# A frozen instruction order, turns on quarters of the array, and a first quad loaded by hardware queues

## The chip, the cores and the metric

The kernel runs on one core of a Trainium2 chip. A core has a matrix engine (TensorE, PE in the profile; PEld is its loading of weights), a vector engine (VectorE, DVE), a scalar engine (ScalarE, ACT), GpSimd (POOL) and SyncE (SP). Each engine works through its own list of instructions in order and waits on semaphores for the others. Data come from memory (HBM) into on-chip memory by DMAs. A DMA is issued either by POOL, through a queue whose descriptors are made in software and which can change fp32 to bf16 on the way, or by SP and ACT, through hardware queues, which copy the numbers as they are. Matrix products land in PSUM, which has eight banks of 128 x 512 fp32 numbers, and are copied out by DVE or ACT.

The metric is the device time of one execution in microseconds (us).

## The reference

```python
def _attn_ref(q, k, v):                      # 8 batches, 12 heads, 448 tokens, 64 numbers per head
    scores = scale * np.matmul(q, k.transpose(0, 1, 3, 2))
    attn = np.maximum(scores, 0.0) ** 2 / S
    return np.matmul(attn, v)

def _moe_ref(x, w_gate, w_val, w_out):       # x is the attention's output, 3584 x 768
    gate = np.maximum(x @ w_gate, 0.0)       # 768 x 1536
    val = x @ w_val                          # 768 x 1536
    return gate * val @ w_out                # 1536 x 768
```

There is no softmax: a score becomes relu(score) squared, and the sum over keys needs no other normalisation. So each block of keys can be finished by itself, and all scale factors move to the end.

## The kernel before

**Attention.** Heads are worked on in quads, four heads of one batch; a batch has three quads (0, 1, 2). Of a quad, queries lie in partitions 0 to 63 of a tile, keys in 64 to 127, with seven slots of 64 tokens each. A *turn* is a transpose on PE (a matrix product with the identity, `ident`) that brings the 64 numbers of a head into the partitions, so that scores can be computed; it lands in PSUM and DVE or ACT copies it to `qkT`. For each slot of keys PE computes the scores of all queries (L686), DVE or ACT takes the relu out of PSUM (L699, L697) and squares it (L711, L709), and PE multiplies by the values (L728); the result goes to `xT` (L744, L746). Products of 64 rows and 64 columns of weights use a quarter of PE's array, and four quarters can work at once.

The first batch is split in two halves of the queries (192 and 256), so that the feed-forward part can begin early. Its quads are turned by L540 (first half of the queries and the keys) and L547 (the other queries), those of batch 1 by L588, 28 turns of 128 tokens' worth of columns per quad with the full 128 partitions as rows, so that query and key slots turn together. Batches 2 to 7 are turned by DMAs on SP's queue, from a rearranged copy (`perm`, L610 or L612).

**Feed-forward.** Batches 0 and 1 use plain products with the gate and value weights (L793). From batch 2 on, pairs of batches use seven products in place of eight (Strassen's scheme in Winograd's form, L902), with sums and differences made on DVE and copies of PSUM (L849 on ACT, L853 on DVE). The output product is done in the same way (L1017, copies L851 and L855), and stored from SP's queue, at the end from ACT's too (L989).

**Loads.** All inputs come through POOL's queue (L404), changed to bf16 on the way; at most eight are under way. Only the first half of the queries of quad 0 of batch 0 comes as fp32 by the hardware queues of ACT and SP (L455) and is changed to bf16 on DVE (L457).

**Order.** While the program is built, a planner (`Planner`, `plan`) decides what each engine does and when. PE's order and that of the loads are written out as strings of letters (`PE_ORDER`, `LOAD_ORDER`); a third string (`AHEAD`) shifts the ranks of DVE's and ACT's operations. The planner prices each operation with costs that are written in the code, takes the one that can start first, and so settles the engine of an operation that DVE or ACT could do, and the bank or buffer of each result. Where its calendar has a hole on PE in the first 32 us, it puts in *fillers*: products of ones (L1171) that nobody reads. An operation's emitted place on its engine is all that remains of the calendar; the chip runs the lists as they stand, with semaphores between them.

Of the kernel before, what the change touches and what calls it, by code (L numbers as in the profile page):

```python
# [15 lines left out]
class Res:  # L16


    def __init__(self, n):
        self.free = {i: 0.0 for i in range(n)}  # L20
        self.by = {}

    def at(self, i):

        t, op = self.free[i], self.by.get(i)
        return t if op is None else max(t, op.end + Planner.LATE[1])


class Buf:


    def __init__(self, res, among=None, width=1):
        self.res, self.width = res, width
        self.among = among if among is not None else sorted(res.free)
        self.readers, self.last, self.idx = 0, 0.0, None

    def pick(self, now=0.0):

        best = None
        for i in self.among:  # L40
            if all(i + w in self.res.free for w in range(self.width)):
                t = max(self.res.at(i + w) for w in range(self.width))
                if best is None or max(t, now) < max(best[0], now):
                    best = (t, i)
        return best


class Op:


    def __init__(self, engs, emit, deps=(), alloc=(), reads=(), mode=None, grp=None):
        self.engs, self.emit = engs, emit
        self.deps, self.alloc, self.reads = list(deps), list(alloc), list(reads)
        self.mode, self.grp = mode, grp
# [4 lines left out]
        self.start = self.end = self.eng = None  # L59
        for b in self.reads:  # L60
            b.readers += 1


class Planner:
    NOUT = 8
    SWITCH = 0.1
    BIAS = 0.2
    MARGIN = 1.5
    LATE = (2.0, 1.0, 0.3)
    TO_LOAD, LOADED = 2.35, 0.95  # L70
    TO_TURN, TURNED, TURN = 1.7, 0.8, 3.65
    ISSUE = 0.28
    TO_HW = 1.9
    COLD = 4.6, 1.6
    FILL_FROM = 0.4
    FILL_COLD = 5.5
    FILL_UNTIL = 32.0
    FILL_MARGIN = 0.1
    GV_ORDER = '1256734'
    OUT_ORDER = 'ab1cd572364'  # L80
    END_ORDER = ('517364', '523')
    BUFFERS = (3, 11, 3, 4, 4, 4, 3)
    PV_PAIRS = (0, 0)
    JOIN = True
    TWO_QUEUES = True
    SPLIT = False
    MERGE = False
    URGENT = {'sh': -0.5, 'perm': 0.5}
    YIELD = {'sq': 0.1, 'sh': 0.1}
    PV_AT_0 = 0  # L90
    QT = 3
    PART = 6
    PV_AT = (1, 1)
    T_AT = (1, 1)
    MORE_UNTIL = 6
    BY_PE = 6
    ORDER = 'LV610ab2c3x4oy5rzqp'

    def __init__(self, banks):
        self.banks = banks  # L100
        self.t = {"POOL": 1.25, "DVE": 0.85, "ACT": 0.74, "SP": 0.74}
        self.ops = []
        self.mode = None
        self.dma_t = 0.0
        self.queues = [], []
        self.loads = []

    def free_at(self, bank):
        return self.banks.free.get(bank, 1e9)

    def now(self, op):
        return self.t.get("PE", 0.0) if "PE" in op.engs else 0.0

    def ready(self, op):
        r = 0.0
        for d in op.deps:
            if d.end is None:
                return None
            if d.eng != "PE" or "PE" not in op.engs:
                r = max(r, d.end + (self.LATE[0] if d.xbar else self.LATE[2] if d.load else 0.0))  # L120
        for b in op.alloc:
            p = b.pick(self.now(op))
            if p is None:
                return None
            r = max(r, p[0])
        return r

    def best(self, op):
        r = self.ready(op)
        if r is None:  # L130
            return None
        c = None
        for e, (occ, busy) in op.engs.items():
            if e in ("DVE", "ACT"):
                r = max([r] + [d.end + self.MARGIN for d in op.deps if d.load and not d.hw])
            s = max(r, self.t.get(e, 0.0))
            if e == "PE" and op.mode != self.mode:
                s = max(r, self.t.get(e, 0.0) + self.SWITCH)
            f = s + busy + (self.BIAS if e == "DVE" and len(op.engs) > 1 else 0.0)
            if c is None or f < c[0]:  # L140
                c = (f, s, e)
        return c[1], c[2], r

    def rates(self, a, b):

        if not (a and b):
            return 1.0, 1.0
        share = a[0][0].share
        return 1.0 - share, share

    def flow(self, a, b, t, until):
        while t < until and (a or b):
            rates = self.rates(a, b)
            d = min([q[0][1] / r for q, r in zip((a, b), rates) if q] + [until - t])
            t += d
            for q, r, post in zip((a, b), rates, (self.LOADED, self.TURNED)):
                if q:
                    q[0][1] -= d * r
                    if q[0][1] < 1e-6:
                        q.pop(0)[0].end = t + post  # L160
        return t

    def transfer(self, queue, op, arrival, work):


        self.dma_t = max(self.flow(*self.queues, self.dma_t, arrival), arrival, self.dma_t)
        self.queues[queue].append([op, work])
        self.flow(*([list(x) for x in q] for q in self.queues), self.dma_t, 1e9)

    def commit(self, op, s, e):  # L170
        assert op.behind is None or op.behind.start is not None
        op.start, op.eng = s, e
        occ, busy = op.engs[e]
        if e == "PE" and s < self.COLD[0] and op.kind != "fill":
            occ, busy = occ * self.COLD[1], busy * self.COLD[1]
        now = self.now(op)
        self.t[e] = s + occ
        op.end = s + busy
        if e == "PE":
            self.mode = op.mode  # L180
        if op.hw:
            self.transfer(0, op, s + self.TO_HW, op.load)
        elif op.load:
            self.loads.append(op)
            self.transfer(0, op, s + (op.to or self.TO_LOAD), op.load)
        elif op.xbar:
            self.transfer(1, op, s + self.TO_TURN, self.TURN)
        else:
            op.end += op.land
        for b in op.alloc:  # L190
            t, b.idx = b.pick(now)
            assert t <= s + 1e-6
            for w in range(b.width):
                del b.res.free[b.idx + w]
                b.res.by.pop(b.idx + w, None)
            b.last = op.end
        for b in op.reads:
            b.readers -= 1
            b.last = max(b.last, op.end + (self.LATE[1] if op.land or op.xbar else 0.0))
            if b.readers == 0:  # L200
                for w in range(b.width):
                    b.res.free[b.idx + w] = b.last
                    if op.xbar:
                        b.res.by[b.idx + w] = op
        self.ops.append(op)
# [3 lines left out]
PE_ORDER = (  # L209
    'aaaccdabaabcbdafjabbaebbbaacdfhafcBBADDaabbabgaZLBKMBAccabaGCFFFCFFdagbaJJebjHHbbaAEFaadEcaaGBCBAAggcbaAFLDGFA'  # L210
    'PGGbaaCCCACgfcccBEbbaGEEDACedcccCCbbaDAfgAbbacBDCaaAAAhccbCCbaBCAaAadBeAabacBJbaDBACBDGcBFAAFAACBHAAGBAFBBCBAA'
    'BDfaAADaaCCAAcBBABaaABBAacbabDAGDAEABBCAIEAEACABAAcACbaAACAGAabbBABaaBCADAecbEACAaAFebaBACEAabEEFAfaBFgaCAabdA'
    'CbbaGBAdeCBecdCAaaaAAAABaebaAEKADBAQCBADADABAAAbaDBAbbBDAAACacFBAaabFBACCGCCABcbaCDBAADEbbaEABCAIBBAdIAAbdHFAA'
    'CaaDACCCaJACBABCBBfbaBABaccAACADbaAAAAadaaICAcaAAaaABAaabaBBbaaCEIACaFKBAAJABBAACABAAABCBBBACBCDCBAABAAAADADHC'
    'BDCBICHABCFBHACAFEBEHBABCAEGBBDBBDCCECAAAGBABBABBBCGEAABBCBCCBABBABBBA'
)
LOAD_ORDER = (
    'aaaaaafcbaakaacaaedbbbthbcabkacccefhbdiggaggaacddaaeebfdbecaccacabfdebcgagbaaeabhabddeaacejejafacacaammkbddbbf'
    'dacabba'
)  # L220
AHEAD = (
# [7 lines left out]
    'iirisnnpmtmbhgjmliojiqibnfpmqnlhmqlkrqirmgnrkbhgmfkfhiinjolmbgnpgnrmjpouoqjmdqqivtssxbolmfhoqpqtqnnligsktopkqu'  # L229
    'kminsgnsiljkjruqjolqoplphilpnnigmrljomgnipnnpismjkkoqnlkpgikmkmknkjingpnqkmojsnklmkjrqmpmklhgknllfrlgqkjknmlfj'  # L230
    'nrrmpslmrmnnnikmonninkjmmmqjlikpqqmnjohpijopklkn'
)

def arranged(ops, letters, base):

    left, out = list(ops), []
    for c in letters:
        out.append(left.pop(ord(c) - ord(base)))  # L240
# [1044 lines left out]
```

## Time and profile before

| | |
|---|---|
| runs | 403.94, 406.0 and 1019.69 us; median 406.0 |
| span of the profiled execution, first to last instruction | 402.3 us |
| own time of the profiled execution | not listed apart from the span; the runs shown at 403.94 and 406.0 lie 1.6 and 3.7 us above it |
| PE busy | 393.8 us, 98% |
| DVE busy | 326.1 us, 81% |
| ACT busy | 274.0 us, 68% |
| POOL busy | 75.7 us, 19% |
| bytes moved by DMA | 43.54 MB, mean 108 GB/s |
| mean granted clock of PE | 0.990 |

The run of 1019.69 us lies far outside and is left out of what follows.

How to read the profile: the span runs from the first to the last instruction. A busy time is the time in which an engine has at least one instruction running; PE's instructions overlap, so a busy PE is not a PE at its peak. The clock row gives the share of PE's full clock that was granted in each fortieth of the span. The chain that ended last is followed back from the last instruction, at each step to what released it. In a table of stretches each row gives start and end, length, busy time of each engine with the number of its instructions, the granted clock, the mean busy share of the 16 DMA engines, and GB/s.

### The profile page before, as it was taken

To read this page: it belongs to the slowest core of one execution; us is meant where nothing else is said; L and a number is where in the kernel's file an instruction comes from. 1 tells how busy PE (TensorE), PEld (TensorE's weight loads), DVE (VectorE), ACT (ScalarE), POOL (GpSimd) and SP (SyncE) were. 2 spreads that over 40 slices of the span, in tenths; PEclk is the share of its full clock that TensorE was granted. 3 is DMA by queue.
4 is the path that set the end of the run, shared out by engine and by line. 5 is a ranking of instruction groups with operands and counts; after the bars stand their busy time and mean duration, and the time that the engine had idled before them with its cause. 6 is when DMAs were issued, how large, how long until landed. Compare 5 with 4: busy or idle time off the path is not lost.

```text
span 402.3 us, 8737 instructions
## 1 busy us (share of the span) xinstructions
PE 393.8 (98%) x3472; PEld 210.1 (52%) x3472; DVE 326.1 (81%) x568; ACT 274.0 (68%) x399; POOL 75.7 (19%) x121
## 2 busy tenths in 40 slices
PE   6999999999999999999999999999999999999995
PEld 3567745454455554444455554444555555555563
DVE  5688788999989879969988989888789967758662
ACT  3697786477979728969879868878788843333221
POOL 7946441020430110311030221300100000000000
PEclk9799999999999999999999999999999999999999
DMA  8999999948988995193698796682224320000245
GB/s 121 192 198 199 201 193 183 147 48 136 124 144 171 162 116 115 26 145 56 84 141 153 152 131 129 82 92 47 46 37 99 80 59 2 0 0 2 59 118 139
DMA packets 77337, 43.54 MB, mean 108 GB/s; under 512 B 40688, under 2 KB 77296, under 8 KB 77296
## 3 DMA queue, kind: packets, MB, share of 16 engines
q0 software_dynamic: 34640, 23.50, 43.1%
q1 hardware_dynamic: 42192, 18.98, 26.5%
q8 instruction: 27, 0.44, 0.5%
q10 hardware_dynamic: 464, 0.49, 0.4%
q14 instruction: 14, 0.11, 0.1%
HBM read 47.19 MB, written 11.01 MB: 145 GB/s over the span
## 4 chain that ended last, share of the span: by engine, by line
PE 95%; DMA 1%; DVE 1%; POOL 0%; issue 0%; ACT 0%; POOLq 0%
PE ps L902 36%; PE ps L1017 25%; PE ps L793 14%; PE ps L686 10%; PE ps L728 8%; DMA gvT<-in_q_dram 1%; PE ps L1171 1%; PE ps L540 1%; PE ps L588 1%; DVE at L711 1%; POOL gvT L404 0%; DVE at L699 0%; DVE qkT L515 0%; DVE f L853 0%; ACT xT L744 0%
## 5 line engine op out<-in xcount | busy, mean ns | idle before, releaser
L697 ACT ACTIVATE at<-ps 128x896 bf16<-128x896 f32 (+4 forms) x116 | 103.2, 906 | 22.6 <-PE ps L686 21.8
L849 ACT COPY f<-ps 128x448 f32<-128x448 f32 x99 | 52.1, 532 | 45.8 <-PE ps L902 34.2
L709 ACT ACTIVATE at<-at 128x896 bf16<-128x896 bf16 (+1 forms) x72 | 67.0, 947 | 2.0 <-DVE at L699 1.2
L711 DVE TENSOR_TENSOR at<-at 128x896 bf16<-128x896 bf16 (+4 forms) x99 | 58.9, 607 | 9.2 <-ACT at L697 8.1
L699 DVE TENSOR_SCALAR at<-ps 128x896 bf16<-128x896 f32 (+4 forms) x55 | 58.4, 1064 | 6.9 <-PE ps L686 6.2
L404 POOL DMA_DIRECT2D vv<-in_v_dram x44 | 26.7, 611 | 165.5 <-PE ps L686 152.5
L686 PE MATMUL ps<-qkT 64*64 64x448 bf16 (+2 forms) x756 | 51.5, 342 | 1.0 <-ACT xT L744 0.3
L902 PE MATMUL ps<-xT,gvT 128*128 128x448 bf16 x216 | 50.9, 353 | 0.0
L902 PE MATMUL ps<-sx,wv 128*128 128x448 bf16 x216 | 50.6, 353 | 0.1
L902 PE MATMUL ps<-xT,wg 128*128 128x448 bf16 x216 | 49.7, 353 | 0.0
L902 PEld LDWEIGHTS <-gvT 128*128 128x128 bf16 x324 | 30.7, 98 | 30.5 <-issue 3.2
L1017 PEld LDWEIGHTS <-sh 128*128 128x128 bf16 x312 | 29.5, 98 | 22.9 <-issue 3.6
L1017 PEld LDWEIGHTS <-hT 128*128 128x128 bf16 x270 | 25.3, 98 | 20.5 <-issue 4.5
L1017 PE MATMUL ps<-wo,hT 128*128 128x384 bf16 x192 | 35.6, 327 | 0.0
L686 PEld LDWEIGHTS <-qkT 64*64 64x64 bf16 x756 | 19.5, 106 | 27.5 <-issue 22.4
L728 PE MATMUL ps<-at,vv 64*64 64x448 bf16 (+2 forms) x700 | 33.4, 327 | 0.0
L1007 DVE SCALAR_TENSOR_TENSOR o<-ps,f 128x384 f32<-128x384 f32 x41 | 22.5, 554 | 12.1 <-PE ps L1017 7.2
L902 PEld LDWEIGHTS <-wv 128*128 128x128 bf16 x216 | 20.6, 98 | 21.0 <-issue 2.8
L793 PE MATMUL ps<-xT,wv 128*128 128x448 bf16 (+2 forms) x180 | 31.3, 316 | 0.0
L902 PEld LDWEIGHTS <-wg 128*128 128x128 bf16 x216 | 20.6, 98 | 19.9 <-issue 1.7
L851 ACT ACTIVATE f<-ps 128x384 f32<-128x384 f32 x37 | 18.2, 491 | 18.6 <-PE ps L1017 18.3
L793 PE MATMUL ps<-xT,wg 128*128 128x448 bf16 (+2 forms) x180 | 30.6, 315 | 0.0
(72 smaller groups left out, 495.5 us busy)
## 6 DMA issues: line engine op xcount, KB each, us to landing
out_dram<-o SPq DMA_DIRECT2D x108, 96.0 KB, 2.2
vv<-in_v_dram POOLq DMA_DIRECT2D x44, 112.0 KB, 5.1
raw<-in_k_dram POOLq DMA_DIRECT2D x18, 224.0 KB, 5.4
raw<-in_q_dram POOLq DMA_DIRECT2D x18, 224.0 KB, 6.0
wo<-in_moe_w_out_dram POOLq DMA_DIRECT2D x4, 576.0 KB, 16.7
wg<-in_moe_w_gate_dram POOLq DMA_DIRECT2D x5, 384.0 KB, 9.9
wv<-in_moe_w_val_dram POOLq DMA_DIRECT2D x5, 384.0 KB, 10.6
gvT<-in_k_dram POOLq DMA_DIRECT2D x5, 224.0 KB, 6.3
```

Source lines behind the costliest of these rows:

```text
L404: op = Op({"POOL": (0.5 + 0.0004 * n_desc,) * 2}, lambda: nc.gpsimd.dma_start(out=dst(), in_=src), deps=deps, alloc=alloc)
L686: nc.tensor.matmul(banks()[64 * j:64 * j + 64, z, h2], lhsT=self.k_of(j, h2, k), rhs=self.q_of(j, h2), start=True, stop=True)
L697: nc.scalar.activation(self.at_of(i, m), banks(), AF.Relu)
L699: nc.vector.tensor_scalar_max(self.at_of(i, m), banks(), 0.0)
L709: nc.scalar.activation(a, a, AF.Square)
L711: nc.vector.tensor_tensor(a, a, a, ALU.mult)
L728: nc.tensor.matmul(ps[64 * h2:64 * h2 + 64, ps2.idx + j, :n], lhsT=st.v_of(j, h2, c), rhs=self.at_of(c)[64 * j:64 * j + 64, 0, h2], start= ...
L793: nc.tensor.matmul(ps[:, pb.idx, z * n:(z + 1) * n], lhsT=w[:, kd, fc], rhs=xT_t[xbuf[b].idx][:, kd, cols], start=(kd == 0), stop=(kd == K ...
L849: nc.scalar.copy(dst, src)
L902: nc.tensor.matmul(ps[:, pb.idx, :S], lhsT=w(g)[:, fc], rhs=rhs, start=start and g == 0, stop=stop and g == KH - 1, skip_group_check=True)
L1007: op = Op({"DVE": V384}, lambda: nc.vector.scalar_tensor_tensor(o_t[ob.idx], ps[:, pb.idx, :OH], float(out_scale), f_t[fb.idx][:, :OH], AL ...
L1017: nc.tensor.matmul(ps[:, pb.idx, :OH], lhsT=lhs(kf), rhs=rhs(kf), start=start and kf == 0, stop=kf == FH - 1, skip_group_check=True)
```

## The change

**The order.** The planner, its costs and its three strings go. A string `PLAN` stands in their place: for every operation its number, the engine if there is a choice, and the bank or buffer of each result; `replay` emits the operations in that order. Fillers stand in the string too, with bank, number and width. The order of all engines, the choice between DVE and ACT and the buffers differ from before all through the kernel.

**The turns.** Every turn on PE is now one of 64 x 64: a slot of queries or of keys of one head. A quad of batch 1 takes 56 instead of 28, and the order in `transpose_pe` alternates between queries (partitions 0 to 63) and keys (64 to 127). Results go to two separate banks, one for queries and one for keys, instead of a pair. For the first batch the keys are turned first, into one bank for each pair of heads, then the queries.

**The first quad.** Keys (all seven slots) and the first half of the queries of quad 0 come as fp32, by two loads each, on the queues of ACT and SP, and are changed to bf16 by DVE or ACT. POOL's queue begins with the keys of quad 1.

```diff
-    op = pe(emit, 0.93, deps=st.qk_ops + [id_op], alloc=[ps2, st.qt_buf], mode="128x64")
+    def turn(bank_of, st, a, slots, js=(0, 1), shift=0):
+        for t in slots:
+            for j in js:
+                for h2 in range(2):
+                    pb, c = bank_of(a, j)
+                    nc.tensor.transpose(ps_b[64 * h2:64 * h2 + 64, pb.idx, c + (t - shift) * P2:c + (t - shift + 1) * P2],
+                                        st.raw()[64 * a:64 * a + 64, 2 * j + h2, t, :],
+                                        ident[64 * a:64 * a + 64, 64 * a:64 * a + 64])
...
+        def emit():
+            for t in range(NT):
+                for a in range(2):
+                    turn(lambda a, j: (pbs[a], j * S), st, a, (t,))
+        op = pe(emit, 0.47, deps=st.qk_ops + [id_op], alloc=[*pbs, st.qt_buf], mode="64x64")
...
-            k_op = dma_in(lambda: st.raw()[64:128, hs], src(k)[:, hs], 128, 0.05)
-            ld = Op({eng: (0.65, 0.65)}, lambda: queue.dma_start(out=wide[0:64, hs], in_=src(q, 0, QT)[:, hs]))
-            cv = Op({"DVE": (0.46, 0.55)}, lambda: nc.vector.tensor_copy(st.raw()[0:64, hs, :QT], wide[0:64, hs]), deps=[ld])
+        def piece(x, rows, j, slots, eng, queue, us, act):
+            ld = Op({eng: (0.65, 0.65)}, lambda: queue.dma_start(out=wide[rows, hs, :slots], in_=src(x, 0, slots)[:, hs]))
+            cv.emit = lambda: copy_out(cv.eng, st.raw()[rows, hs, :slots], wide[rows, hs, :slots])
...
+        two = (("ACT", nc.scalar), ("SP", nc.sync))
+        st.k_ops = [piece(k, slice(64, 128), j, NT, *two[j], 3.5, True) for j in range(2)]
+        st.q_ops = [piece(q, slice(0, 64), j, QT, *two[j], 3.55, True) for j in range(2)]
...
-    for op in plan(first, att, ffn, others, pool_ops, still_op, filler, r_ps):
-        op.emit()
+    replay([*sum(first, []), *att, *[o for o, _ in ffn], *others, *pool_ops], filler)
...
+def replay(ops, filler):
+    while True:
+        i = number(2)
+        if i == FILL:
+            filler(number(), number(), number(2))
+            continue
+        op = ops[i]
+        op.eng = list(op.engs)[number() if len(op.engs) > 1 else 0]
+        for b in op.alloc:
+            b.idx = number()
+        op.emit()
```

The scores, the products of the feed-forward part, their shapes and their numbers stay as they are.

More of the change, by code (lines that the diff above doesn't have):

```diff
@@ L19, in __init__ @@
     def __init__(self, n):
[L20 to L26, printed above, removed]
+        self.n = n
 class Buf:
-    def __init__(self, res, among=None, width=1):
+    def __init__(self, res, width=1):
         self.res, self.width = res, width
[L34 to L45, printed above, removed]
+        self.idx = None
 class Op:
-    def __init__(self, engs, emit, deps=(), alloc=(), reads=(), mode=None, grp=None):
+    def __init__(self, engs, emit, deps=(), alloc=(), reads=(), mode=None):
         self.engs, self.emit = engs, emit
         self.deps, self.alloc, self.reads = list(deps), list(alloc), list(reads)
-        self.mode, self.grp = mode, grp
+        self.mode = mode
         self.load = self.land = self.share = 0.0
@@ L58, in __init__ @@
         self.xbar = 0
[L59 to L120, printed above, removed]
-        for b in op.alloc:
[L122 to L205, printed above, removed]
@@ L389, with bank, bank2, both @@
     A896, V896 = (0.83, 0.98), (1.0, 1.13)
-    PAIRS, MORE_PAIRS, FIRST_PAIRS = [0, 2, 4, 6], [0, 2, 4, 6], [0, 2, 4, 6]
-    SINGLES = [7, 6, 5, 4, 3, 2, 1, 0]
-    def bank(among=None):
-        return Buf(r_ps, among if among is not None else SINGLES)
-    def bank2(among=None):
-        return Buf(r_ps, among if among is not None else PAIRS, width=2)
+    def bank():
+        return Buf(r_ps)
+    def bank2():
+        return Buf(r_ps, width=2)
+    def both(pair):
+        return ps[:, pair.idx:pair.idx + 2, :]
     others, pool_ops = [], []
@@ L1074, in out_both @@
         rest = None
-        if Planner.JOIN and b == B - 4:
+        if b == B - 4:
             keep()
@@ L1160, with filler @@
     others.extend([still_op, id_op])
-    def filler(us, cold):
-        pb = bank([7, 6, 5, 4, 3, 2, 1, 0])
-        total = int(us * (1200 if cold else 2400))
-        n = (total + S - 1) // S
-        width = max(64, total // n)
-        def emit():
-            for _ in range(n):
-                nc.tensor.matmul(ps[:, pb.idx, :width], lhsT=still[:, :128], rhs=still[:, :width], start=True, stop=True)
-        op = Op({"PE": (us, us)}, emit, deps=[still_op], alloc=[pb], reads=[pb])
-        op.kind = "fill"
-        return op
+    def filler(bank, n, width):
+        for _ in range(n):
+            nc.tensor.matmul(ps[:, bank, :width], lhsT=still[:, :128], rhs=still[:, :width], start=True, stop=True)
     for g in range(NQ):
@@ L1197 @@
             load_gv(1, 2)
[L1198 removed]
+        elif x == "0":
             load_gv(0, 1)
```

381 lines of the change are left out of this document (168 added, 213 removed).

## The prediction

> **What bounds it now.** I read the busy shares and the clock row first, then the chain that ended last, then tables of stretches.
>
> ```profile
> span 402.3 us, 8737 instructions
> PE 393.8 (98%) x3472; PEld 210.1 (52%) x3472; DVE 326.1 (81%) x568; ACT 274.0 (68%) x399; POOL 75.7 (19%) x121
> PEclk9799999999999999999999999999999999999999
> ```
>
> PE is busy 98% of the span, but the third slice (10 to 20 us) was granted 0.7 of the clock. Stretches (us, then busy of PE, PEld, DVE, ACT, POOL, then granted clock, DMA share, GB/s):
>
> ```profile
> 8.88:15.70 6.82, 6.64 (x87) 3.60 (x87) 3.53 (x8) 3.50 (x5) 5.95 (x9) 0.50 1.38 192
> 15.70:27.60 11.90, 10.69 (x289) 7.40 (x289) 10.25 (x19) 10.53 (x16) 7.83 (x11) 1.00 1.50 194
> 7.33:27.60 20.27, 18.35 (x395) 11.46 (x396) 15.20 (x29) 15.00 (x22) 14.12 (x21) 0.83 1.44 193
> 27.60:398.20 370.60, 370.39 (x3038) 196.48 (x3038) 307.23 (x526) 257.21 (x376) 55.30 (x87) 1.00 0.67 103
> ```
>
> From 27.60, the first feed-forward product, to 398.20 PE idles 0.2 us: there the time is PE's work. Before 27.60 it is not: PE's busy time holds fillers and, from 8.88 to 15.70, half a clock. The chain in order of time (start, us, what) shows the start:
>
> ```profile
> 1.25 1.91 POOL gvT L404 x3
> 3.15 5.77 DMA gvT<-in_q_dram
> 9.06 1.53 PE ps L540 x19
> 11.80 1.47 PE ps L540 x21
> 14.07 1.86 PE ps L1171 x5
> 27.60 2.58 PE ps L793 x30
> 30.63 0.90 PE ps L588 x28
> 239.41 0.64 DVE f L853
> 398.20 0.56 DVE o L1007
> ```
>
> POOL's issues, the landing of quad 1's queries (8.9), turns, fillers (L1171), feed-forward. Each entry is what was late. So the change can gain in three places: before 27.60, in PE work that goes away, and in lost beats of the dense part. For the last I compare the start-to-start time of each pair of neighbours on PE after 27.60 with the median of its kind (189 ns between products of 448 columns, 163 for 384, 282 where the array changes shape): what lies above adds up to **1.0 us**, 0.29 of it at the wait for a DVE copy at 239.41. No more is to be won there.
>
> **The change, part by part**
>
> *Start.* Quad 0's keys leave POOL's queue, so its issue of quad 1's keys moves from 2.54 to 1.25 and all behind it by 1.3 us. The keys come instead as two fp32 loads of 224 KB on the ACT and SP queues, next to the two of 96 KB that stood there. DMA issues, KB each, us to landing:
>
> ```profile
> gvT<-in_k_dram POOLq DMA_DIRECT2D x2, 112.0 KB, 3.8
> hT<-in_q_dram SPq DMA_DIRECT2D x1, 96.0 KB, 3.3
> hT<-in_q_dram ACTq DMA_DIRECT2D x1, 96.0 KB, 3.5
> ```
>
> A 224 KB load is not in the trace. From below it lands like the 96 KB one, 4.1; from above all 640 KB run first from 2.3 at the 208 GB/s that the stretch 3.00 to 4.00 shows, 3.1 us, plus 0.8 to the semaphore: 6.2. I take 5.2 for the later keys. Then come the casts (a 64x384 cast on DVE took 348 ns, so 64x896 takes 0.6 to 0.8; on ACT the nearest row is the 128x896 cast, 905 ns), the queries' cast 0.35, seven pairs of turns 0.25, and two copies of 0.4: scores at 5.2+0.7+0.35+0.25+0.8 = 7.3, against 7.33 now. So quad 0 gains nothing (-1.1 to +1.0). Behind the new waits stands all of PE (it waits now too, to 4.65 and 6.41), and on ACT and DVE nothing that could run. ACT's two issues (0.73 each) push its 1.28 us table load to end at 3.5, still before any landing.
>
> Quads 1 and 2 are what gains: their queries landed at 8.93 and 10.58 and were the chain; 1.3 less each. From 7.33 to 27.60 DVE and ACT work 15.2 and 15.0 us of 20.3, idle mostly at half clock (3.3 each). The same scores (84 of 192 columns, 76 of 256) stand ahead of the first feed-forward product in both orders, so the floor is half of their sum, 15.1, plus 0.3 for smaller and more copies: 7.3+15.4 = 22.7, i.e. **-4.9**. From above: the new order gains nothing, 0. I take the first product at 24.2, **-3.4**: 1.3 from the queue, 1.5 because turns (3.0 us in the chain at half clock) and the filler of 1.86 shrink, 0.6 from a denser order. Weights do not forbid it: the first ones landed at 17.7 and 19.9, and the products of 27.5 to 30 used theirs 4.5 to 7.6 us after landing.
>
> *Turns of batch 1.* Three times 28 turns of 128 columns (0.90 each) become 56 of 64 columns on 64x64 quarters. Group row (busy, mean ns) and timeline row (start, us):
>
> ```profile
> L547 PE MATMUL ps<-ident,gvT 64*64 64x64 bf16 x48 | 1.1, 193 | 0.4 <-DVE at L699 0.4
> 16.96 0.69 PE L547 MATMUL ps<-ident,gvT 64*64 64x64 bf16 x32 [0.41 <-DVE at L699]
> ```
>
> 32 such turns start within 0.69-0.19 = 0.50 us, 16 ns each, but on two quarters of the array; the new ones alternate between both halves of the partitions. If four run at once, as in attention times values (28 products of 448 columns in 1.32 us in the chain, 47 ns each, a quarter of 189), it is 8 ns: 56 x 8 = 0.45, with 0.1 more until the next product starts (it starts 150 ns after the last of the 28 turns) 0.55. If not, 56 x 16 + 0.1 = 1.0. So -0.35 to +0.1 each; I take -0.35, the row with four quarters at work being the nearer one: **-1.05** (-1.05 to +0.3). The turns of quads 0 to 2 (40 x 16 = 0.64 at full clock) cost what they cost now.
>
> [...]
>
> *Order.* Switches of array shape after the first product: 64 pairs now, 65 then: nothing. DVE and ACT trade: 12 relus go to ACT (1.086 on DVE, 0.917 on ACT), 16 copies of 448 (0.616 on DVE, 0.532 on ACT) and 17 of 384 go to DVE. DVE becomes about 9 us busier, ACT 6 less busy. Both lie under PE (307 and 257 of 370.6); what it costs without the cover is a rival below. Of the 1.0 us I take **0** (-1.0 to +4, the lower price of that rival less its gain). SP's and POOL's later queues keep their operations in another order; POOL idles 165 us before its value loads, cover enough. *End.* Same last operations: last copy, two issues, landing: 4.1 us in both.
>
> **Sum**: -3.4-1.05 = -4.45; span 402.3-4.45 = 397.9. Of the runs shown, 403.94 and 406.0 (the median) lie 1.6 and 3.7 above this span; with the middle, 2.6, that is **400.5 us**, 1.4% under the median.
>
> **Rivals**
>
> *The start runs at its floor* (0.30): -4.9 before the first product, and up to -1.3 more if one and a half groups of two scores (relu 1.03 and square 0.68 us each) may still wait in their banks then, split over two engines; middle -5.5. With -1.05 and 0.8 of the 1.0: -7.35, 395.0+2.6 = **397.5**. For it: DVE and ACT are 87% busy from 15.70 on, so only the hole before it has to close. Against: the values for quads 0 to 2 landed up to 18.8 and come only 1.3 sooner.
>
> *The clock stays at half until feed-forward* (0.10). Stretches of all, then of the turns L540 alone:
>
> ```profile
> 8.88:12.29 3.41, 3.23 (x48) 1.82 (x50) 1.76 (x5) 1.99 (x3) 3.00 (x5) 0.50 1.37 189
> 12.29:15.70 3.41, 3.41 (x43) 1.78 (x43) 1.77 (x4) 1.51 (x2) 2.95 (x5) 0.50 1.38 196
> 8.88:12.29 3.41, 2.26 (x38) 1.58 (x40) 0.50 1.37 189
> ```
>
> PE was busy 3.23 us, 2.26 of them turns, and the clock did not rise; after the next stretch, with 1.70 us of fillers, it did. The new order has 22 fillers instead of 34 and none once scores of quad 2 run. If it stays low for four more stretches of 3.41, 13.6 us, PE loses 6.8; idle and fillers of 15.70 to 27.60 (1.2+2.8) absorb 4.0. Net +2.8, the gain at the start is lost, turns -1.05: 404.1+2.6 = **407**, slower. It decides when a stretch holds less other work than some value between 1.0 (8.88 to 12.29, turns aside) and 2.1 (15.70 to 19.11, 2.82 busy with 0.69 of turns, clock kept). [...]
>
> *Copies on DVE come late* (0.14). At 239.41 one of nine 448-column copies on DVE held PE up, by 0.29 us; there are 25 now, each behind DVE's queue. If the 16 new ones do so, +4.6; if each also waits for one more operation of 0.62 on DVE, 16 x 0.91 = +14.6, and 412.4+2.6 = **415**. It decides where DVE's queue is longer than PE's lead over the bank.
>
> *The gains don't appear* (0.06): 16 ns turns (+0.3), start as now: 402.6+2.6 = **405**.
>
> **Chances.** The forecast 0.40. A measurement of this kernel can tell about 2% from no change, 8 us: under 397.9 is faster, over 414 slower. Faster: 0.20 of the first rival, whose price lies at that bound, and 0.06 of the forecast's lower side. Slower: half of the copies' 0.14, and 0.01 of the clock's with nothing absorbed. Range 394.5 to 410: below, the floor with all of its terms, -6.2-1.05-1.0, is a span of 394.0, and the lowest run lies 1.6 above its span, less 1 us between runs; above, the clock's rival with 3 us of its cover gone.
>
> **What would show it.** First feed-forward product at about 24.2, granted clock 1.00 or 0.50 in each stretch to 27, blocks of 56 turns 0.55 us, quad 1's queries landing at 7.6, and PE's idle time after the first product under 1 us. Wrong if the product comes after 26, if turns start 16 ns apart, or if PE's waits for DVE copies grow past 3 us.

## The result, and the profile after

The changed kernel took **415.04 us** (median of four runs, 414.18 to 415.96) against 403.94 for the kernel before (403.26 to 406.0, median of three; a fourth, disturbed run of 1019.69 is left out). The ratio is **1.027**, 95% interval 1.023 to 1.032: 2.7% slower. The forecast was 400.5 us in a range of 394.5 to 410, so the prediction is wrong, and on the wrong side. The profiled execution has a span of 414.0 us, where 397.9 was forecast and the kernel before had 402.3.

The page of the changed kernel: span, busy shares, clock row, and the chain that ended last, by engine and by line.

```profile
span 414.0 us, 8953 instructions
PE 394.4 (95%) x3580; PEld 209.2 (51%) x3580; DVE 329.3 (80%) x593; ACT 264.8 (64%) x378; POOL 74.5 (18%) x119
PEclk9999999999999897999999999999999999999999
PE 85%; DMA 6%; DVE 3%; SPq 2%; ACT 1%; issue 1%; DVEq 0%
PE ps L721 35%; PE ps L836 20%; PE ps L612 14%; PE ps L506 8%; PE ps L547 6%; DMA out_dram<-o 4%; SPq L452 2%; DMA hT<-in_k_dram 1%; ACT at L516 1%; DVE at L518 1%; PE ps L364 1%; DVE at L530 1%; PE ps L981 1%; SPq L808 1%; DVE qkT L352 0%
```

PE's busy time hardly grew, but the span did: PE idles 19.6 us, where it idled 8.5. The clock row shows two new low digits, in the 14th and 16th slice (134 to 166 us); that it shows none at the start is no reading, as told below. And the chain holds something that a kernel bound by PE should not have: **output stores** (`out_dram<-o`, 4%) and DMA transposes (L452, 2%).

Stretches of the changed kernel that answer to those of the prediction (us, then busy of PE, PEld, DVE, ACT, POOL, granted clock, DMA share, GB/s); the first feed-forward product now starts at 26.79 and PE ends at 409.75:

```profile
8.88:15.70 6.82, 6.82 (x147) 3.82 (x147) 3.95 (x10) 4.16 (x7) 6.82 (x10) 1.00 1.46 193
15.70:26.79 11.09, 8.59 (x267) 6.24 (x264) 10.68 (x21) 11.09 (x18) 6.95 (x11) 1.00 1.41 199
26.79:409.75 382.96, 373.54 (x3118) 196.34 (x3117) 310.54 (x549) 246.80 (x352) 54.27 (x86) 0.99 0.66 100
```

The start gained 0.74 us, not 3.4. The 1.00 in the first of these rows is not a measurement: the trace has no record of the clock before 13.97 us, and the table prints 1.00 where there is none. The fillers show the clock. The same four stand ahead of the first scores in the changed kernel (first row) and in run 5 below, where the record begins with full clock at 5.08 us (start, us, what):

```profile
8.75 1.46 PE L981 MATMUL ps<-woT 128*128 128x384 bf16 x4
5.85 0.82 PE L990 MATMUL ps<-woT 128*128 128x384 bf16 x4
```

They start 320 ns apart in the one and 163 in the other. So the clock of the changed kernel stood at half until 13.97 us, and was full from there to the first product. And the dense part, where PE used to idle 0.2 us, now has 9.4 us without a product.

The start-to-start count of the prediction, made on the new trace, gives the account. Before: first product 27.53 (27.60 in the merged chain that the prediction shows), lost beats 0.96, the rest of PE's work 369.67, and 4.16 behind the last product. After: 26.79, **14.42**, 368.55, 4.26. So the clean work shrank by 1.1 us, as forecast, the start by 0.74, and 13.5 us came in as lost time: 3.38 at 134 us, 4.07 at 151, 2.0 at 32, and 3.8 while the clock stood at half (136.85 to 140.26 and 153.91 to 160.74, 10.2 us; PE stood idle in the holes for 2.6 of them, and half of the rest is 3.8).

What each engine waited for between 125 and 160 us in the changed kernel (us in total, times, longest):

```profile
DVE o L674 <- DMA out_dram<-o: 5.0, 1, 5.0
DVE o L826 <- DMA out_dram<-o: 4.6, 1, 4.6
ACT f L668 <- DVE o L826: 4.5, 1, 4.5
PE ps L721 <- DVE f L672: 3.9, 1, 3.9
PE ps L721 <- DVE o L826: 3.2, 1, 3.2
```

The chain of the same stretch (start, us, what):

```profile
127.17 2.04 SPq L452
...
129.89 7.01 DMA out_dram<-o
...
137.02 0.57 DVE o L826
...
137.63 1.28 PE ps L721 x3
...
143.59 1.82 SPq L452
...
146.11 7.70 DMA out_dram<-o
...
153.93 0.56 DVE o L674
...
155.01 0.62 DVE f L672
...
155.68 5.48 PE ps L721 x15
```

It reads in order of time. SP issues a pair of DMA transposes, then a store. The store lands after 7.0 us. DVE waits for that landing, 4.6 us, to write its next output tile, because there are only four and all hold values not yet stored. DVE works in a fixed order, so its next copies and operand sums stand behind that wait, and PE stands behind those. It happens twice. The feed-forward product at 155.68 is named as waiting for a DVE copy (L672), but this copy took 0.62 us; it was late because it stood behind L674.

Late stores are not new. DMA issues between 125 and 150 us, KB each, median us to landing, in the kernel before:

```profile
out_dram<-o SPq DMA_DIRECT2D x18, 96.0 KB, 5.6
qkT<-perm SPq DMA_TRANSPOSE x4, 7.9
```

and in the changed kernel:

```profile
out_dram<-o SPq DMA_DIRECT2D x15, 96.0 KB, 5.7
qkT<-perm SPq DMA_TRANSPOSE x4, 8.3
```

The same delays. But the waits of the kernel before list none of DVE's for a store: behind its first pair of transposes it filled four tiles and asked for the next at 141.65, just after the first of them had landed (141.21), and behind the second pair PE ran sixty feed-forward products, which need no output tile (chain, start, us, what):

```profile
143.53 11.48 PE ps L902 x60
```

The new order wants a tile 4.6 and 5.0 us before one is free.

### The profile page after: what moved, and what is told of

The parts are those of the page before. It is cut to its first block, busy times and chain, and to the rows that moved or that the text cites. A ratio compares the mean times of both kernels' runs of the same rounds, so it can differ in the third digit from the quotient of the medians.

```text
span 414.0 us, 8953 instructions
## 1 busy us (share of the span) xinstructions
PE 394.4 (95%) x3580; PEld 209.2 (51%) x3580; DVE 329.3 (80%) x593; ACT 264.8 (64%) x378; POOL 74.5 (18%) x119
## 4 chain that ended last, share of the span: by engine, by line
PE 85%; DMA 6%; DVE 3%; SPq 2%; ACT 1%; issue 1%; DVEq 0%
PE ps L721 35%; PE ps L836 20%; PE ps L612 14%; PE ps L506 8%; PE ps L547 6%; DMA out_dram<-o 4%; SPq L452 2%; DMA hT<-in_k_dram 1%; ACT at L516 1%; DVE at L518 1%; PE ps L364 1%; DVE at L530 1%; PE ps L981 1%; SPq L808 1%; DVE qkT L352 0%
## 5 line engine op out<-in xcount | busy, mean ns | idle before, releaser
L516 ACT ACTIVATE at<-ps 128x896 bf16<-128x896 f32 (+2 forms) x126 | 111.2, 915 | 29.0 <-PE ps L506 28.5
L668 ACT COPY f<-ps 128x448 f32<-128x448 f32 x83 | 43.3, 534 | 53.8 <-PE ps L721 26.3
L528 ACT ACTIVATE at<-at 128x896 bf16<-128x896 bf16 (+3 forms) x71 | 65.0, 940 | 2.1 <-DVE at L518 1.6
L721 PE MATMUL ps<-xT,gvT 128*128 128x448 bf16 x216 | 52.0, 360 | 3.9 <-DVE f L672 3.9
L518 DVE TENSOR_SCALAR at<-ps 128x896 bf16<-128x896 f32 (+4 forms) x45 | 46.9, 1045 | 11.0 <-PE ps L506 7.1
L506 PE MATMUL ps<-qkT 64*64 64x448 bf16 (+2 forms) x756 | 52.9, 342 | 2.1 <-ACT at L516 1.4
L721 PE MATMUL ps<-sx,wv 128*128 128x448 bf16 x216 | 51.8, 359 | 0.0
L836 PEld LDWEIGHTS <-sh 128*128 128x128 bf16 x312 | 29.7, 99 | 24.2 <-issue 4.7
L547 PE MATMUL ps<-at,vv 64*64 64x448 bf16 (+2 forms) x700 | 33.8, 327 | 2.2 <-issue 1.9
L612 PE MATMUL ps<-xT,wv 128*128 128x448 bf16 (+2 forms) x180 | 30.3, 316 | 0.0
L836 PE MATMUL ps<-wo,sh 128*128 128x384 bf16 x156 | 30.3, 333 | 0.0
```

The costliest lines, as they stand in the source:

```text
L506: nc.tensor.matmul(banks()[64 * j:64 * j + 64, z, h2], lhsT=self.k_of(j, h2, k), rhs=self.q_of(j, h2), start=True, stop=True)
L516: nc.scalar.activation(self.at_of(i, m), banks(), AF.Relu)
L518: nc.vector.tensor_scalar_max(self.at_of(i, m), banks(), 0.0)
L528: nc.scalar.activation(a, a, AF.Square)
L547: nc.tensor.matmul(ps[64 * h2:64 * h2 + 64, ps2.idx + j, :n], lhsT=st.v_of(j, h2, c), rhs=self.at_of(c)[64 * j:64 * j + 64, 0, h2], start= ...
L612: nc.tensor.matmul(ps[:, pb.idx, z * n:(z + 1) * n], lhsT=w[:, kd, fc], rhs=xT_t[xbuf[b].idx][:, kd, cols], start=(kd == 0), stop=(kd == K ...
```

## The experiments

**1. Seven output tiles.** One of the three xT tiles holds nothing until 157 us; it serves as three more output tiles for the fourteen that are filled between 117 and 157 us. The order stays.

```diff
+OUT_TILES = '01234561324513'
+    spare = xT_t[0].rearrange("p k s -> p (k s)").bitcast(FP32)
+    o_t += [spare[:, OH * i:OH * (i + 1)] for i in range(3)]
-    r_x, r_f, r_g, r_o = Res(N_X), Res(N_F), Res(N_G), Res(N_O)
+    r_x, r_f, r_g, r_o = Res(N_X), Res(N_F), Res(N_G), Res(len(o_t))
...
             b.idx = number()
+            if b.res.n == 7:
+                b.idx = int(next(out_tiles, b.idx))
```

> The changed kernel, with seven output tiles instead of four for the fourteen tiles filled between 117 and 157 us (the three more lie in the third xT tile, which holds nothing until then); order, engines and everything else are kept. Theory A (stores that land late hold the output tiles, the vector engine waits for one in its fixed order, TensorE waits behind it, and its clock falls to half after each hole): both holes (3.4 and 4.1 us) and the 5.1 us at half clock go, so the span falls from 414.0 to about 401.5 and the ratio to the kernel before is 0.99 to 1.005. Theory B (the vector engine has too much work in this order, the wait for the tile only hides it): the holes shrink by less than half, span above 409, ratio above 1.015.

Measured: 404.78 us against 403.4 for the kernel before on the same chip, ratio 1.003 (0.9996 to 1.0064). The page of this run:

```profile
span 402.7 us, 8952 instructions
PE 389.9 (97%) x3580; PEld 208.2 (52%) x3580; DVE 329.6 (82%) x593; ACT 264.9 (66%) x378; POOL 74.5 (19%) x119
PEclk9999999999999999999999999999999999999999
```

Stretches of the changed kernel around the holes, with the columns of above:

```profile
135.00:140.00 5.00, 2.37 (x8) 1.00 (x8) 2.98 (x6) 2.23 (x3) 0.00 (x0) 0.68 0.28 80
150.00:155.00 5.00, 1.77 (x10) 0.79 (x9) 1.02 (x2) 0.60 (x2) 0.00 (x0) 0.89 1.03 173
155.00:160.00 5.00, 4.32 (x12) 1.72 (x12) 2.80 (x6) 2.12 (x2) 1.24 (x2) 0.50 0.93 112
```

and of the run with seven tiles:

```profile
135.00:140.00 5.00, 5.00 (x54) 2.72 (x52) 4.97 (x11) 3.18 (x5) 2.08 (x4) 1.00 0.61 160
150.00:155.00 5.00, 5.00 (x28) 2.61 (x27) 4.21 (x8) 1.75 (x4) 1.24 (x2) 1.00 0.88 141
155.00:160.00 5.00, 5.00 (x38) 2.20 (x37) 4.61 (x8) 3.74 (x5) 0.00 (x0) 1.00 0.45 84
```

Both holes and both falls of the clock are gone and the span is 11.3 us shorter, though the stores still landed after 4.2 and 4.8 us (median of the stores of the two kinds of tiles). Theory A holds, B falls: with the wait for the tile away, the vector engine kept up. Set beside the changed kernel product by product, this run wins 7.4 us in the two holes and 3.8 in the stretches at half clock; the expectation had 5.1 for the second, since it counted the idle part of them twice. The lost time after the first product is 3.32 us; without the stop at 32 us, which is still there (2.27), it is 1.05, as in the kernel before.

**2. No loads beside the transposes.** What delays the stores? This run leaves out fifteen loads that POOL issues from 118.9 to 158.2 us.

```diff
-        op.emit()
+        if i not in SKIP:
+            op.emit()
```

> The changed kernel without the fifteen loads of keys, queries and values that POOL issues between 118.9 and 158.2 us; the attention of the quads they belong to works on what lay in the tiles before. The two pairs of DMA transposes at 125.7 and 142.3 us and the stores behind them stay. Theory H (loads that run beside a DMA transpose stretch it from 2.2 to 6 and 7.6 us, and the stores behind it on the same queue wait it out): the transposes land within 3.5 us, the stores within 3.5 us, and the two holes of 3.4 and 4.1 us fall to under 0.5 us together; span 401 to 404. Theory I (two transposes ahead of a store are enough): stores still land after 4 to 6 us, and more than 2 us of holes stay; span 406 to 412.

DMA issues between 125 and 150 us of this run:

```profile
out_dram<-o SPq DMA_DIRECT2D x19, 96.0 KB, 2.2
qkT<-perm SPq DMA_TRANSPOSE x5, 3.6
```

From the end of its issue a transpose landed within 2.2 to 2.3 us, a store within 1.6 to 1.8; the holes were gone and the span of its one execution was 402.1. Theory H, not I: with no load beside them, two transposes ahead of the stores left these at 2.2 us in the median, which is also the median of all 108 in the changed kernel.

**3. No DMA transposes.** The same edit with the two pairs of transposes in the list.

> The changed kernel without the two pairs of DMA transposes issued at 125.7 and 142.3 us; their two quads work on the queries and keys that lay in the tiles before. The loads and stores stay. Theories H and I (a transpose ahead of the stores is what delays them): stores between 129 and 150 us land within 3.7 us, as those at 117 to 124 us did beside loads alone, both holes go, span 401 to 404. Theory J (the loads alone delay the stores): stores still land after 5 us and more, the holes stay above 5 us together, span above 408.

The holes went and the span of its one execution was 403.7. From the end of their issue most stores landed after 1.6 to 4.2 us; two at 126.7 and 127.3, behind loads alone, took 5.0 and 4.7, and two at 140.0 and 140.6 took 4.2, more than the 3.7 expected. So J falls as the cause of the holes, but beside loads alone stores were late too, by up to 5.0 us. Only with both, transposes on the store's queue and loads beside them, did DVE wait 4.6 and 5.0 us for one of four tiles.

**4. Fillers in the holes.** Is the half clock a cost of its own?

```diff
+HOLD = {300: [(3, 16)], 306: [(0, 19)]}
+        for bank, n in HOLD.get(i, ()):
+            filler(bank, n, 448)
         op = ops[i]
```

> The changed kernel, with 16 and 19 idle matmuls of 448 columns (3.0 and 3.6 us at 0.189 us) put before the two feed-forward products that wait at 134 and 151 us; they write a free bank and nothing reads it. Theory C (the half clock after each hole, 3.4 and 6.8 us long, is the gate's answer to the idle time): the clock stays full, the 27 beats of 0.374 us return to 0.189, and the span falls by 4 to 5 us, to 409 to 410 (ratio 1.012 to 1.018). Theory D (the slow beats come from elsewhere): span 414 or more, ratio 1.025 to 1.035.

Granted clock in this run, same columns:

```profile
135.00:140.00 5.00, 4.83 (x29) 2.54 (x26) 2.97 (x6) 2.25 (x3) 0.00 (x0) 1.00 0.28 80
150.00:155.00 5.00, 4.87 (x26) 2.42 (x25) 0.56 (x1) 0.14 (x1) 0.00 (x0) 1.00 0.94 182
155.00:160.00 5.00, 3.81 (x21) 1.98 (x21) 3.89 (x7) 2.33 (x3) 1.24 (x2) 1.00 0.49 107
```

The clock stayed at 1.00 in these stretches, where the changed kernel had 0.68, 0.89 and 0.50, so in these two places the idle time was the cause of the half clock (theory C as far as that goes). But the price was wrong. The half clock had cost 3.8 us, not 5.1, and not all of it came back: at 166 us PE was 2.0 us ahead of the changed kernel, not 4 to 5, because the second hole ends when a store lands, and whoever gets there sooner waits longer (3.59 us of fillers and 1.49 more, against 4.07). At the end 0.9 us were left, after another wait for an output tile at 237 us, and the timed ratio, 1.033 (1.027 to 1.038), is no better than that of the changed kernel. So curing the clock alone gave 2.0 us; the 3.8 that run 1 won there need the holes gone too.

**5. The first keys by POOL.**

```diff
+        for cv in st.k_ops:
+            cv.deps[0].emit = cv.emit = lambda: None
+        def by_pool():
+            for j in range(2):
+                hs = slice(2 * j, 2 * j + 2)
+                nc.gpsimd.dma_start(out=st.raw()[64:128, hs], in_=src(k)[:, hs])
+        st.k_ops[0].deps[0].emit = by_pool
```

> The changed kernel, with the keys of the first quad loaded and cast by POOL's queue in two pieces ahead of its other loads, as in the kernel before; its first queries still come as fp32. Theory S (the fp32 keys, the second piece of which landed at 7.20 us, set the start): the first scores go from 10.14 back to about 7.3 us and the first feed-forward product from 26.8 to 24 to 25 us; the time is 1.8 to 2.8 us shorter (ratio to the kernel before 1.020 to 1.023). Theory T (what sets the first feed-forward product is the work of the vector and scalar engines and the supply of instructions after 14 us): first scores earlier but first product at 26 to 27.5 us, time within 0.8 us of the changed kernel (1.025 to 1.030).

First scores at 6.60 instead of 10.14 us, first feed-forward product at **23.81** instead of 26.79, ratio 1.0209 (1.0157 to 1.0262). Theory S. The keys are not all of the 3.0 us, since the clock was full here from 5.08 to 15.32 us and at half in the changed kernel until 13.97. Two later executions are nearer to each other: both have one stretch of 3.41 us at half clock ahead of the first product, run 6 with the fp32 keys (8.94 to 12.35 us) and the second execution of run 8 with the keys by POOL (16.75 to 20.16), and their first products come at 26.21 and 24.09. By that pair the keys are worth some 2 us; that the rest is the clock's is not shown. At 46 us, 1.8 of the 3.0 us were left: the clock had stood at half again from 32.39 to 35.80. At the end it was 4.3, since this run reached the two holes earlier and they were shorter (2.88 and 3.30 us).

**6. Wide turns.** The stop at 32 us, 1.9 us in the changed kernel and 2.2 in run 1. The chains name it "issue": PE waits for nothing that the profile shows.

```diff
-            for t in range(NT):
-                for a in range(2):
-                    turn(lambda a, j: (pbs[a], j * S), st, a, (t,))
+            for j in range(2):
+                for t in range(NT):
+                    for h2 in range(2):
+                        nc.tensor.transpose(ps_b[64 * h2:64 * h2 + 64, pbs[j].idx, t * 128:(t + 1) * 128],
+                                            st.raw()[:, 2 * j + h2, t, :], ident)
```

> As the run with seven output tiles, and the three turn blocks of batch 1 with 28 wide turns each (queries and keys together) instead of 56 narrow ones, as in the kernel before: 56 instructions fewer in each block. Theory F (the 2.2 us hole at 32.25 us is TensorE waiting for its next 256 instructions, whose fetch starts only when it enters the block before; the hole sits at the 1216th instruction whatever stands there): the hole shrinks to 0.3 to 1.2 us and moves later, the blocks cost 0.35 us more each, so the time is within 1 us of the run with seven tiles. Theory G (the hole is a wait for data of the operation that stands there): it stays at 2.2 us before the same matmul, and the time is 1.0 us above that run.

The stop was gone (PE never stood idle for more than 0.29 us from the first product until 213 us), which goes further than F said and excludes G. Until 200 us PE was 1.1 us ahead of run 1; then waits of 1.9 us for output tiles came in at 213 to 228 us, where only four tiles exist in both. Timed: 1.006 (1.0024 to 1.0095) against 1.003 (0.9996 to 1.0064), not told apart.

**7. Forty instructions more.** The direct test of F: 20 idle matmuls of 8 columns while PE waits for its first data.

```diff
+            if first:
+                filler(7, 20, 8)
+                first = False
             filler(number(), number(), number(2))
```

> The kernel with seven output tiles, with 20 matmuls of 8 columns (40 instructions with their weight loads) before its first fillers, while TensorE waits for its first data; nothing reads what they write. In the run without them TensorE stopped before its 704th, 960th and 1216th instruction, for 1.23, 0.29 and 2.27 us, the last at the 45th of 56 probability-value matmuls, at 32.02 us. Theory F (instructions arrive 256 at a time): the stops stand at the same counts, so 20 matmuls earlier in the work (the last after about 25 of the 56), end at the same times within 0.5 us (34.3 us the last), and the span grows by 0.3 to 1.5 us from 402.7. Theory G (the operation there waits for data): the last stop stands at the 45th matmul again, and the span is 402.7 within 0.5.

The chain of run 1 at the stop:

```profile
30.98 1.31 PE ps L552 x45
32.28 2.21 issue
34.49 0.54 PE ps L552 x11
```

and of this run (the line of the same matmul is 555 here):

```profile
31.14 0.76 PE ps L555 x25
31.91 0.72 issue
32.63 1.09 PE ps L555 x31
```

After 45 of 56 matmuls in one, after 25 of 56 in the other: **the stop stands at a count of instructions, not at an operation**. That is F; G falls. Its length and its end were not as expected (0.72 us, at 32.6 instead of 34.3): PE passed the earlier instructions sooner (the 1024th at 29.2 instead of 30.4 us), and the packet on the instruction queue (last section) began sooner, at 30.2 instead of 31.9. A further stop of 1.1 us came in at the 1472nd instruction. The span, 404.3, holds 1.3 us of waits for output tiles at 215 and 228; up to 200 us this run was 0.1 behind run 1.

**8. All three together.** Ten output tiles (three more from another free xT tile between 215 and 245 us), keys by POOL, wide turns.

> Three edits together on the changed kernel: three more output tiles in each of the two stretches 117 to 157 and 215 to 245 us (in xT tiles that hold nothing then), the first quad's keys by POOL's queue, and wide turns for batch 1. By the runs before: seven tiles gave 11.3 us, keys by POOL 1.8 us past the start, wide turns 1.1 us; the stall on output tiles at 213 to 228 us that cost 1.9 us in the run with wide turns should go. If they add up, the span is 414.0 - 11.3 - 1.8 - 1.1 = 399.8, the time 401 to 402 and the ratio 0.993 to 0.998. If the keys and the wide turns repair the same delay (the loads that both wait for at 35 us), only one of the two counts and the ratio is 0.998 to 1.003.

401.09 us against 402.89, ratio **0.9955** (0.9929 to 0.9981). Once more, beside the last two runs:

> The run with all three edits once more, beside the two runs that change one thing of it: ratio to the kernel before 0.993 to 0.998.

400.91 against 403.82, ratio 0.9924 (0.9892 to 0.9957). The page of this second run:

```profile
span 398.8 us, 8781 instructions
PE 389.7 (98%) x3496; PEld 209.0 (52%) x3496; DVE 328.8 (82%) x592; ACT 264.1 (66%) x377; POOL 75.9 (19%) x121
```

Both times it beats the kernel before, by 0.5 and 0.8%, and the changed kernel by more. From the first product (24.09) to its end PE stands idle for 0.3 us, where the changed kernel has 9.4 and the kernel before 0.2.

**9. The same, keys as fp32, but first.** SP issues its half of the keys before its half of the queries.

```diff
         i = number(2)
+        i = {633: 629, 629: 633}.get(i, i)
```

> As the run before, but the keys stay fp32 on the hardware queues, and SP issues its half of the keys ahead of its half of the queries instead of behind it. Theory S (the start waits for the second half of the keys): this half lands at about 5.5 instead of 7.2 us, the first scores come 1 to 1.7 us earlier than at 10.1, and the time lies 0 to 1.5 us above that of the run with keys by POOL. Theory U (the sum of fp32 bytes on the queues sets it, in whatever order): the last piece needed still lands at about 7 us, first scores at 9.5 to 10.2, and the time is 1.5 to 2.5 us above that run.

402.98 us, ratio 1.0002 (0.998 to 1.0024), 1.9 above run 8. The last piece of the keys landed at 5.55 us (S), but the last piece of all at 7.40 (U), and the first scores came at 8.89: between the two. Order helps by 1.2 us of the 3.0 to 3.4 that keys by POOL give. The time, 1.9 above run 8, is U's; whether the bytes on these queues, the casts behind them or the clock (at half from 9.24 to 12.65 us here) cost the rest was not taken apart.

**10. The same as 8, with narrow turns.** The edit of run 6 taken back.

> The run with all three edits (keys by POOL, ten output tiles, wide turns), but with the narrow turns left as in the changed kernel. Theory N (the narrow turns' shorter blocks are worth what the prediction gave them, 0.35 us each): the time is 0.8 to 1.1 us below that of the run with all three. Theory F (they double the instructions of a block, and TensorE runs out at the 1216th): a stop of 1.5 to 2.3 us at about 29 us, and the time 0.5 to 1.5 us above it.

401.54 us (400.11 to 402.59) against 400.91 (400.4 to 402.56) for run 8 on the same chip, ratios 0.9952 and 0.9924: not told apart. Its profiled execution was 0.8 us shorter and had a stop of 0.73 us at the same 1216th instruction. Neither theory's number came; narrow turns are worth nothing that these runs resolve. Its first product was the earliest of all, 22.60, and 3.7 us later PE waited 0.76 us for weights that landed at 26.97: the loads, which the prediction had ruled out as a limit for a first product at 24.2, begin to hold one at 22.6.

**11. Fewer fillers.**

```diff
-            filler(number(), number(), number(2))
+            bank, n, width = number(), number(), number(2)
+            if first:
+                filler(bank, n, width)
+                first = False
```

> The run with all three edits, without the last 11 of its 22 filler matmuls (4, 1, 4 and 2 of 384, 440, 392 and 224 columns; 22 instructions in all), which fill TensorE's gaps between 7 and 16 us. Theory F: the stop at the 704th instruction (2.0 us at 17.27 us in the run with all three) comes 11 matmuls later and is 0.2 to 0.5 us shorter; time 0 to 0.5 us less. Theory C (idle time costs the clock): the clock falls to half somewhere between 8 and 24 us, and the time is 0.5 to 4 us more.

Stretches of this run:

```profile
10.00:15.00 5.00, 3.11 (x110) 2.85 (x109) 4.79 (x10) 3.84 (x6) 4.41 (x7) 0.50 1.33 187
15.00:20.00 5.00, 4.80 (x128) 4.11 (x128) 3.74 (x8) 4.38 (x8) 4.61 (x7) 0.62 1.50 177
20.00:25.00 5.00, 2.58 (x56) 2.27 (x59) 3.18 (x6) 2.82 (x4) 2.48 (x3) 0.72 1.39 197
```

Theory C: the clock was at half from 8.52 to 18.75 us and again from 22.17 to 25.58 (in the second execution of run 8 from 16.75 to 20.16 alone), the first product came at 26.89 instead of 24.09, and the time was 402.18, 1.3 above run 8. The stop at the 704th instruction did not shrink as F would have it: 2.4 us, against 2.0 in the first execution of run 8.

## Why the prediction was wrong, point by point

Forecast and measured spans lie 16.1 us apart: 11.2 in the dense part between 133 and 161 us, 2.6 before the first product, 2.0 at the stop at 32 us, and 0.3 elsewhere.

- **Order, "I take 0 (-1.0 to +4)": failed, 11.2 us.** The step priced DVE's and ACT's shares and passed over SP's queue in half a sentence ("keep their operations in another order"); it counted idle time of POOL as the cover. Nobody asked how long an output tile stays taken. Run 1 shows that this alone, with the half clock that followed, was the loss. The kernel before gave both numbers: four output tiles, and stores that took 5.6 us to land behind transposes. Missing was the question of what DVE does while they are out.
- **"Later keys at 5.2", "scores at 7.3": failed, 2.6 us at the first product.** The keys landed at 7.20, above the upper bound of 6.2. That bound let the 640 KB of the hardware queues run first; but POOL's load of quad 1's keys, 224 KB, issued at 1.24 and landed at 5.54, ran beside them. With it the same sum gives 2.3 + 864 KB / 208 GB/s + 0.8 = 7.25. The 0.8 to the semaphore is an estimate that no view shows; here the last packet of these keys ended at 6.87, 0.33 before they landed. That this is how the 7.20 came about is not shown: from 2.5 to 7 us the changed kernel moves 207 to 294 GB/s, POOL's later loads among them. (The trace did hold loads of 224 KB, contrary to what the step says, but on POOL's queue: 6.3 us in the median.) Behind the keys the sum had 2.1 us to the scores, and it was 2.9: the copies were done at 9.34, but four fillers stood ahead on PE, at half clock, until the first scores at 10.14. Run 5 takes the keys off and gets a first product at 23.81, near the 24.2 forecast; run 10 reached 22.60, the floor of 22.7 that the first rival named. So the gain was there; the fp32 keys, and beside them the half clock, spent it.
- **Quad 1's queries at 7.6:** right, 7.43.
- **Turns, 0.55 a block:** right, 0.50 from the first turn to the next product in each of the three, 8.6 to 8.8 ns a turn, about half of the 16 ns that L547 shows before, which fits four quarters at work instead of two. What was missed is that 28 instructions became 56, each with a weight load: the gain of 1.1 to 1.3 us over three blocks came, and 2.0 were lost at the stop (runs 6 and 7).
- **Rival "the clock stays at half":** came in part. The clock stood at half until 13.97 us, from the first fillers on (408 columns, 340 ns apart from 1.70 us, the same per column as the 320 ns for 384 above), where the kernel before had it full from 5.46 to 8.88 and at half until 15.70. From 13.97 to the first product it was full: it rose 1.7 us earlier than before, not 13.6 us later as the rival priced. Afterwards it fell where the prediction had no term, after the holes. That turns count for less than other work, as the rival's bound has it, is the author's estimate from the stretches of before; no run here shows it by itself.
- **Rival "copies on DVE come late", 415 us:** the time is right by luck, for the cause is not. PE did wait 3.9 us for a copy, the sign that was named; but with more output tiles the 25 copies cost nothing (run 1).
- **"Wrong if the product comes after 26":** it did, and rightly showed the second failure. No sign was named for the first and larger one.

## What to carry to other kernels

When a change gives a new order, list for each small pool of buffers what releases it, and where that is a store or another DMA, price the wait by the slowest landings of the trace (here 7 us), not by the usual ones (2.2). A row that says an engine waited for a copy names the last link only: see what the copying engine did just before. And halving the size of an instruction doubles their number: here 28 turns became 56, and a stop of 2.0 us came at the 1216th instruction that was not there with 28 (run 6).

## What was not expected of the hardware

**PE's stops stand 256 instructions apart.** The page of the changed kernel, DMA queues (packets, MB, share):

```profile
q8 instruction: 28, 0.46, 0.4%
```

and of the kernel before:

```profile
q8 instruction: 27, 0.44, 0.5%
```

28 packets of 16 KB beside 2 x 3580 instructions of PE, and 27 beside 2 x 3472: 256 and 257 for each packet. No view says what the packets hold; that they are PE's instructions is read from these counts. Up to 41 us they began 6 to 7 us apart in the changed kernel (12.9, 19.8, 26.0, 32.1 and 38.1 us), the second to the fifth 1.4 to 3.0 us after PE had passed its 512th, 768th, 1024th and 1280th instruction. The stops of this kind, in the changed kernel and the runs after it, stood before PE's 448th, 704th, 960th, 1216th or 1472nd instruction, 256 apart, and it went on 1.2 to 1.6 us after the end of a packet (changed kernel: at 22.33 us after a packet that ended at 20.72, at 34.45 after one that ended at 33.00). Read as theory F has it, a stop is as long as PE is early, and bursts of small instructions (112 of a narrow turn block in 0.48 us) make it early. Why a packet begins later in one run than in another stays open, and with it why the same stop cost 0.7 us in one run and 2.2 in another.

**DMA transposes landed later beside loads.** Beside loads they landed up to 7.6 us after their issue, without them after 2.2 to 2.3 (run 2). The two stores behind them on the same queue that stand in the chain of the changed kernel took 7.0 and 7.7 us; in run 2 the stores took 1.6 to 1.8.

**The clock fell after stretches in which PE still worked.** In the 3.41 us before the first fall, 133.44 to 136.85, PE worked 1.0 us, and in those before the second, 150.50 to 153.91, 1.3; 3.41 and 6.83 us at half clock followed. With fillers in the holes (run 4), or without the holes (run 1), it stayed full there.
